# The output product by Strassen's identity over pairs of batches, in a phase of its own

## The chip, the core and the metric

The kernel runs on one core of a Trainium2 chip. TensorE (PE) multiplies; VectorE (DVE), ScalarE (ACT) and GpSimd (POOL) do the element-wise work; SyncE (SP) issues the DMA transfers. The metric is the device time of one execution in microseconds, as the median of several runs.

## The reference

An attention between 8 batches of 512 tokens and 32 state rows makes 4,352 rows of 512, which go through two gated feed-forward blocks:

```python
def _moe_ref(x, w1, w2, w3, w_out):
    a = x @ w1
    b = x @ w2
    h = a * b @ w3
    return (h @ w_out).astype(np.float32)

def _moe2_ref(x, w_in, w_out):          # w_in 512 x 2048, w_out 2048 x 512
    h = x @ w_in
    relu6 = np.clip(h + 3.0, 0.0, 6.0)
    g = h * relu6 / 6.0
    return (g @ w_out).astype(np.float32)
```

The change is in the second block: `h = x @ w_in` is the hidden product, `g` the gates, `g @ w_out` the output product. All of it is float32. Each factor is split into a rounded part and the rest (`rnd` on ACT, `rest` on DVE or POOL), and a product is three matmuls: high by high, high by low, low by high.

## The kernel before

**Three stages.** A first stage unpacks weights and begins the attention; then one slot after another (`slot`, 8 a batch) makes the first block's rows, which go to DRAM as `x2d[b]`, 512 channels by 512 tokens. In the first batches of this stage `stream2` unpacks `moe2_w_in` and `moe2_w_out` a little in each slot, and writes split weights to DRAM: `swi`, which is `w_in` as the seven weight combinations of Strassen's identity in eight groups of 128 hidden columns, and `swo`, which is `w_out` as it is. The last stage, from 553.8 us in the trace, is the second block, and the change is about it.

**The second block before.** It works on four pairs of batches, `p`. The 2 x 2 blocks of Strassen's identity are two halves of the hidden columns by two halves of the channels (of `w_in`), and two halves of the channels by the two batches (of `x`). `combos(p)` makes the seven combinations of the activations (`xc`: B11, T1, T2, B21, T3, B22, T4) from four loads `r` of `x2d`, a piece each time that the main loop steps it; for the pairs behind the first, four of the seven `rest` operations run on POOL. For each of 8 groups `n`, seven calls of `prod` (L799) do 6 matmuls of 128x128 by 512 columns each into three banks; ACT and DVE combine them to four blocks of hidden values, and `chain` (L812) makes gates of them: relu on ACT, the gate on DVE, `rnd` on ACT, `rest` on DVE.

**The output product before.** The gates of group `n - 1` are the stationary factor of `out_mm` (L840): for each batch and each quarter of the tokens, 6 matmuls of 512 columns against `wo`, 48 a group. They stand between the products of group `n`, one `out_mm` behind each (`T_`). Each result is added on DVE to an accumulator `oa` in SBUF, and after 8 groups the eight accumulators go to DRAM in rows of 2 KB. Rows of the 256 state rows go along in the last pair (`state_h`, and `out_mm` with `j == "s"`).

**What sets the order.** It is written by hand; every engine takes its instructions in the order of the code, and waits by semaphores. SP takes the DMAs likewise. Two buffers hold each tile of weights; a group's `w_load` and `wo_load` (896 KB twice and 512 KB twice) are issued when a group is done.

Of the kernel before, what the change touches and what calls it, by code (L numbers as in the profile page):

```python
# [7 lines left out]
F32 = mybir.dt.float32  # L8
# [11 lines left out]
def attn_moe_kernel(tc, xt_d, xn_d, bd_d, wa, wb, wc, wi, wo, out):  # L20
# [95 lines left out]
    swo = [[dram.tile([128, 2, 512], F32, name=f"swo{hl}{u}") for hl in "hl"] for u in range(8)]  # L116
# [223 lines left out]
    with tc.manual_schedule():  # L340
# [85 lines left out]
        def stream2():  # L426
# [22 lines left out]
            for i, (src, u) in enumerate(units):  # L449
# [26 lines left out]
                a11, a12, a22, a21 = (w[:, 256 * k:256 * k + 256] for k in range(4))  # L476
                s1, s2, s3, s4 = (cm[:, 256 * k:256 * k + 256] for k in range(4))
# [3 lines left out]
                yield  # L481
# [7 lines left out]
                for hl, t in enumerate((h, l)):  # L489
                    nc.sync.dma_start(out=swi[u][hl].rearrange("p s k f -> p (s k f)"), in_=t.bitcast(F32))  # L490
# [92 lines left out]
        def x2_load(p):  # L583
            if p < B // 2:
                x2r[p] = r = [xb.tile([128, 2, 512], F32, tag=f"r{i}", name=f"r{i}") for i in range(4)]
                for i in range(4):
                    nc.sync.dma_start(out=r[i], in_=x2d[2 * p + i % 2][:, i // 2 * 2:i // 2 * 2 + 2, :])

        def combos(p):

            if p >= B // 2:
                return
            b11, b12, b21, b22 = x2r.pop(p)

            def split(k, x, eng):
                t = xb.tile([128, 2, 2, 512], F32R, tag="xc", name="xc", bufs=8)
                h, l = xc[p, k] = t[:, 0], t[:, 1]
                rnd(h, x, "A")
                rest(l, x, h, eng)

            def minus(out_, a, b):
                nc.vector.tensor_tensor(out=out_, in0=a, in1=b, op=ALU.subtract)
            e = "VP"[p > 0]
            split("B11", b11, e)
            yield
            minus(b11, b12, b11)
            yield
            split("T1", b11, "V")
            yield
            minus(b11, b22, b11)  # L610
            yield
            split("T2", b11, "V")
            yield
            split("B21", b21, e)
            yield
            minus(b12, b22, b12)
            yield
            split("T3", b12, e)
            yield
            split("B22", b22, e)  # L620
            yield
            minus(b21, b21, b11)
            yield
            split("T4", b21, "V")
            if p:
                x2_load(p + 1)
            yield
# [86 lines left out]
        for b in range(B):  # L714
# [20 lines left out]
            for m in range(0 if b else 4, M1):  # L735
# [40 lines left out]
        LAST = NG * (B // 2)  # L776
        wts, wos = {}, {}

        def w_load(n):
            if n <= LAST:  # L780
                wts[n] = [pb.tile([128, 7, 2, 128], F32R, tag=f"w{hl}", name=f"w{hl}", bufs=2) for hl in "hl"]
# [106 lines left out]
        def state_h(n, i):  # L888
            if i == 0:
                ps_s[n] = bank("ps_hs")  # L890
# [153 lines left out]
```

## Time and profile before

| | us |
|---|---|
| median of 3 runs | 1265.66 |
| lowest, highest | 1263.24, 1265.81 |
| the profiled execution: device time | 1263.66 |
| the profiled execution: span from the first to the last instruction | 1261.7 |
| busy in the span: PE, DVE, ACT, POOL | 1225.7, 857.5, 518.5, 32.1 |

The span is 1.96 us shorter than the device time of the same execution. A busy PE is not PE at its peak, since matmuls overlap: how fast they follow each other is read from the chain, where one of 512 columns counts 0.23 us, though its own row says 390 ns. DVE and ACT instructions overlap by some 0.08 us as well; what one costs a full queue is the distance between two starts.

### The profile page before, as it was taken

Reading aid. Unit: us, or ns where it says so; the run is one execution under the profiler, and the core shown is the slowest. Engines: PE = TensorE matmul, PEld = TensorE weight load, DVE = VectorE, ACT = ScalarE, POOL = GpSimd, SP = SyncE. Lnnn points to the kernel's source line nnn. Section 1 sums busy time; section 2 is a strip of 40 time slices with the busy share of each in tenths; the row PEclk is TensorE's granted clock in tenths of the full one; section 3 lists DMA queues with packets and bytes.
Section 4 is the critical chain, followed back from the end, with each engine's and each line's share of the span. In section 5 each row is a group of like instructions: output and inputs, shape, how many; then the busy total and the mean of one; then the engine's idle time right before and its main releaser. Section 6 shows DMA issues by size and latency. Waiting matters only on the chain.

```text
span 1261.7 us, 16840 instructions
## 1 busy us (share of the span) xinstructions
PE 1225.7 (97%) x6784; PEld 970.1 (77%) x6784; DVE 857.5 (68%) x1268; ACT 518.5 (41%) x811; POOL 32.1 (3%) x18
## 2 busy tenths in 40 slices
PE   5989999999999999999999999999999999999997
PEld 2446787777778778778888888888888888888885
DVE  7976877786877642645667947679566697556664
ACT  3434545454654533444333543234423344332330
POOL 0000000000000000000000200002000030000000
PEclk9989999999999999999999999999999999999999
DMA  9751554554554201445525553445624254332223
GB/s 354 277 179 68 204 211 178 203 211 173 200 198 165 101 20 49 149 148 207 183 93 183 201 208 125 150 149 192 235 109 182 94 192 167 135 141 93 92 92 117
DMA packets 49589, 202.67 MB, mean 161 GB/s; under 512 B 9192, under 2 KB 11240, under 8 KB 42856
## 3 DMA queue, kind: packets, MB, share of 16 engines
q1 hardware_dynamic: 48936, 200.56, 43.8%
q8 instruction: 53, 0.87, 0.3%
q10 hardware_dynamic: 576, 1.05, 0.2%
q14 instruction: 24, 0.20, 0.0%
HBM read 160.17 MB, written 41.42 MB: 160 GB/s over the span
## 4 chain that ended last, share of the span: by engine, by line
PE 85%; DVE 10%; ACT 2%; DMA 1%; issue 1%; ACTq 0%; DVEq 0%; SPq 0%
PE ps L804 24%; PE ps_o L88 10%; PE ps_o L90 10%; PE ps_o L89 10%; PE x L88 4%; PE x L89 4%; PE x L90 4%; PE ps_ab L88 4%; PE ps_ab L90 4%; PE ps_ab L89 4%; PE ps_p L360 2%; PE ps_hs L804 2%; PE ps_w L414 1%; PE ps_r L228 1%; DVE ab L508 1%
## 5 line engine op out<-in xcount | busy, mean ns | idle before, releaser
L804 PE MATMUL ps<-xc,wh 128*128 128x512 f32 x896 | 276.1, 390 | 0.0
L808 DVE TENSOR_TENSOR oa<-oa,ps_o 128x512 f32<-128x512 f32 x238 | 163.0, 686 | 157.1 <-PE ps_o L90 156.3
L88 PE MATMUL ps_o<-woh,g 128*128 128x512 f32 x512 | 199.8, 390 | 0.3 <-ACT g L71 0.3
L89 PE MATMUL ps_o<-wol,g 128*128 128x512 f32 x512 | 199.7, 390 | 0.0
L90 PE MATMUL ps_o<-woh,g 128*128 128x512 f32 x512 | 199.6, 390 | 0.0
L804 PEld LDWEIGHTS ps<-xc,wh 128*128 128x128 f32 x896 | 168.3, 188 | 34.8
L804 PE MATMUL ps<-xc,wl 128*128 128x512 f32 x448 | 174.6, 390 | 0.0
L71 ACT ACTIVATE g<-gt 128x512 fp32r<-128x512 f32 x128 | 81.0, 632 | 173.0 <-DVE gt L818 172.9
L88 PE MATMUL x<-abh,w3ph 128*128 128x512 f32 (+1 forms) x288 | 112.4, 390 | 0.0
L90 PEld LDWEIGHTS ps_o<-woh,g 128*128 128x128 f32 x512 | 96.2, 188 | 20.5 <-DVE g L79 0.4
L88 PEld LDWEIGHTS ps_o<-woh,g 128*128 128x128 f32 x512 | 96.2, 188 | 20.1 <-ACT g L71 0.8
L89 PEld LDWEIGHTS ps_o<-wol,g 128*128 128x128 f32 x512 | 96.2, 188 | 19.3
L89 PE MATMUL x<-abl,w3ph 128*128 128x512 f32 (+1 forms) x288 | 109.1, 379 | 0.0
L90 PE MATMUL x<-abh,w3pl 128*128 128x512 f32 (+1 forms) x288 | 109.0, 378 | 0.0
L88 PE MATMUL ps_ab<-Ah,ph 128*128 128x512 f32 x256 | 102.7, 401 | 1.6 <-DVE pl L79 0.9
L90 PE MATMUL ps_ab<-Ah,pl 128*128 128x512 f32 x256 | 100.7, 394 | 1.7 <-DVE pl L79 1.7
L79 DVE TENSOR_TENSOR g<-gt,g 128x512 fp32r<-128x512 f32 x128 | 90.1, 704 | 17.9 <-ACT g L71 15.6
L89 PE MATMUL ps_ab<-Al,ph 128*128 128x512 f32 x256 | 100.6, 393 | 0.0
L804 PEld LDWEIGHTS ps<-xc,wl 128*128 128x128 f32 x448 | 84.1, 188 | 17.6 <-DMA wl<-swil 0.2
L71 ACT ACTIVATE abh<-ab 128x512 fp32r<-128x512 f32 (+1 forms) x72 | 43.7, 608 | 114.7 <-DVE ab L508 114.7
L815 ACT ACTIVATE rl<-c,half 128x512 f32<-128x512 f32 x96 | 69.4, 723 | 32.6 <-DVE c L808 31.2
L79 DVE TENSOR_TENSOR abl<-ab,abh 128x512 fp32r<-128x512 f32 (+1 forms) x72 | 47.4, 658 | 39.9 <-ACT abh L71 39.9
(122 smaller groups left out, 1724.2 us busy)
## 6 DMA issues: line engine op xcount, KB each, us to landing
wh<-swih SPq DMA_DIRECT2D x33, 896.0 KB, 4.6
wl<-swil SPq DMA_DIRECT2D x33, 896.0 KB, 6.4
woh<-swoh SPq DMA_DIRECT2D x33, 512.0 KB, 5.3
wol<-swol SPq DMA_DIRECT2D x33, 512.0 KB, 6.2
out_dram<-oa SPq DMA_DIRECT2D x34, 256.0 KB, 2.4
raw<-in_wb_dram SPq DMA_DIRECT2D x8, 1024.0 KB, 6.3
xr<-in_xt_dram SPq DMA_DIRECT2D x8, 1024.0 KB, 6.4
xn<-in_xn_dram SPq DMA_DIRECT2D x8, 1024.0 KB, 8.1
```

Of the source, the lines that this page charges most:

```text
L71: nc.scalar.activation(out=out_, in_=in_, func=AF.Copy)
L79: e.tensor_tensor(out=out_, in0=in_, in1=hi.bitcast(F32), op=ALU.subtract)
L88: nc.tensor.matmul(ps, lh, rh, start=first, stop=False)
L89: nc.tensor.matmul(ps, lh, rl, start=False, stop=False)
L90: nc.tensor.matmul(ps, ll, rh, start=False, stop=last)
L228: nc.tensor.matmul(ps[h:h + 64, c * NS:(c + 1) * NS], xn[:, t, c * 128 + h:c * 128 + h + 64], e2t[:, t, g, o:o + NS], start=(t == 0), stop ...
L360: nc.tensor.matmul(ps[c][32 * q:32 * q + 32, 256 * i:256 * i + 256], st_t[b][r, 2 * c + j, 32 * k:32 * k + 32], w12[mm // 2, 2 * c + j][r, ...
L414: nc.tensor.matmul(w3_ps[m], t[:, o:o + 128], wout[k], start=k == 0, stop=k == M1 - 1)
L508: nc.vector.tensor_tensor(out=ab[:, :n], in0=psb[:, :n], in1=a[:, :n], op=ALU.mult)
L804: nc.tensor.matmul(ps, u[:, a, k, :], v[:, k, :], start=first and k == 0 and i == 0, stop=k == 1 and i == 2, skip_group_check=not first or ...
L808: nc.vector.tensor_tensor(out=out_, in0=a, in1=b, op=ALU.add)
L815: nc.scalar.activation(out=rl, in_=c, func=AF.Relu, bias=half, scale=1.0 / 6.0)
```

## The change

**Products in two phases.** For each pair the hidden product of all 8 groups comes first (`hidden`), as seven calls of `prod` a group, and its gates stay in SBUF, unsplit, in four tiles `G[k][j]` of 8 x 512 (half `k` of the hidden columns, batch `j`). Then comes the output product (`output`), by the same identity: the 2 x 2 blocks are two halves of the 512 output channels by the two halves of the hidden columns (of `w_out`), and the gates. It goes through 28 steps `v`: seven products `i`, each in four steps `u` of 12 matmuls (two groups of hidden columns by two quarters `q` of 64 channels of either half). Here the weights are stationary, the gates move, and the result is transposed: channels by tokens.

**The gates' combinations.** The four sums of the identity are made in place on DVE, half a tile (2,048 columns) at a time (`t_sum`), and the two parts of a step's gates just before their use (`make`: `rnd` on ACT, `rest` on DVE, 1,024 columns) in a ring of three tiles `hl`. `make(v + 2)` stands behind step `v`; three of the 28 are made in the hidden phase.

**The way out.** At the end of a product (`ended`) DVE combines banks, and transposes 32 x 32 blocks (`put`) into `stg`; four DMAs write it in runs of 256 B. There is no accumulator `oa`.

**The activations.** `combos(p + 1)` runs in the output phase of pair `p`, one piece a step, in two halves of the channels (512 columns each instead of 1,024); each half begins with its load (`x2_load(p, k)`, 2 x 512 KB into the one buffer `r`), at steps 1 and 13. All its `rest` operations are on DVE, none on POOL.

**The weights.** `stream2` treats `w_out` as it treats `w_in`, so `swo` grows from 1,024 to 1,792 columns a group, and is stored by four DMAs a group instead of two. `STEPS` gets one more step in every fourth slot. Weights are loaded in units of 4 and 3 tiles of 256 columns (`w_load`, `w_done`), each with two buffers.

**The state rows.** Their hidden products stay in the last pair's groups, their output products (matmuls of 256 columns) go into steps of four of the seven products there.

The token order in the layout on the host changes with it. The diff, cut:

```diff
-    swo = [[dram.tile([128, 2, 512], F32, name=f"swo{hl}{u}") for hl in "hl"] for u in range(8)]
+    swo = [dram.tile([128, 7, 8, 256], F32, name=f"swo{hl}") for hl in "hl"]
...
-                if src is wo:
-                    rnd(h[:, :1024], w, "A")
-                    rest(l[:, :1024], w, h[:, :1024], "V")
-                    for hl, t in enumerate((h, l)):
-                        nc.sync.dma_start(out=swo[u][hl].rearrange("p k e -> p (k e)"), in_=t[:, :1024].bitcast(F32))
-                    yield
-                    continue
-
...
-                yield
...
                 for hl, t in enumerate((h, l)):
-                    nc.sync.dma_start(out=swi[u][hl].rearrange("p s k f -> p (s k f)"), in_=t.bitcast(F32))
+                    to = swi[u][hl].rearrange("p s k f -> p s (k f)") if src is wi else swo[hl][:, :, u, :]
+                    for at, of, n in ((0, 2, 5), (5, 0, 2)):
+                        nc.sync.dma_start(out=to[:, at:at + n, :],
+                                          in_=t.bitcast(F32)[:, 256 * of:256 * (of + n)].rearrange("p (s e) -> p s e", e=256))
...
-        def x2_load(p):
-            if p < B // 2:
-                x2r[p] = r = [xb.tile([128, 2, 512], F32, tag=f"r{i}", name=f"r{i}") for i in range(4)]
-                for i in range(4):
-                    nc.sync.dma_start(out=r[i], in_=x2d[2 * p + i % 2][:, i // 2 * 2:i // 2 * 2 + 2, :])
+        def x2_load(p, k):
+            r = x2r[p, k] = xb.tile([128, 2, 2, 512], F32, tag="r", name="r")
+            for j in range(2):
+                nc.sync.dma_start(out=r[:, :, j, :],
+                                  in_=x2d[2 * p + j].rearrange("p (h k) f -> p h k f", k=2)[:, :, k, :])
...
+            for k in range(2):
+                x2_load(p, k)
+                yield
+                r = x2r.pop((p, k))
...
+                def split(name, x):
+                    if k == 0:
+                        t = xb.tile([128, 2, 2, 512], F32R, tag="xc", name="xc", bufs=7)
+                        xc[p, name] = t[:, 0], t[:, 1]
+                    h, l = (x_[:, k] for x_ in xc[p, name])
+                    rnd(h, x, "A")
+                    rest(l, x, h, "V")
+
+                def minus(out_, a, b):
+                    nc.vector.tensor_tensor(out=out_, in0=a, in1=b, op=ALU.subtract)
+                split("B11", b11)
...
-                for _ in range(STEPS):
+                for _ in range(STEPS + (m % 4 == 3)):
...
-                    if m == 0:
-                        x2_load(0)
-                    else:
-                        next(first, None)
+                    for _ in range(1 if m == 0 else 4):
                         next(first, None)
...
+        def w_done(u):
+            wu.pop(u)
+            w_load(u + 4)
...
+        def t_sum(i, h):
+
+            a = 4 * h
+            b11, b12, b21, b22 = (G[k][j][:, a:a + 4, :] for k in range(2) for j in range(2))
+            if i == 1:
+                sub(b11, b12, b11)
+            elif i == 2:
+                sub(b11, b22, b11)
+            elif i == 4:
+                sub(b12, b22, b12)
+            else:
+                sub(b11, b21, b11)
+
...
+                if old is not None:
+                    o2, om1, ow = old
+                    prod(o2, ow(A22), X("T4"), False)
+                    w_done(2 * (base + n - 1) + 1)
+                    tick()
+                    c21 = small("c", 3)
...
+                prod(d3, w(S1), X("T1"), True)
+                tick()
+                m5 = small("m5", 2)
+                nc.scalar.copy(out=m5, in_=d3)
+                if with_states and n == 0:
+                    states_split()
+                early(n, 0)
+                prod(d1, w(A12), X("B21"), False)
+                tick()
+                chains.append(chain(d1, [(G[0][0][:, n, :], 0, 512)]))
+                early(n, 1)
+                prod(d2, w(S3), X("T3"), False)
+                tick()
                 c22 = small("c", 3)
...
+                add(c22, d2, m1)
+                add(c22, c22, m5)
+                chains.append(chain(c22, [(G[1][1][:, n, :], 0, 512)]))
...
+        def put(c, q, stg):
+            nc.vector.transpose(out=stg[:, :, q, :], in_=c)
...
+        def out_of(p, eh, j, stg):
+
+            blk = 2 * p + j
+            for g in range(4):
+                e = 128 * g + 64 * eh
+                nc.sync.dma_start(
+                    out=out[blk * ROWS:blk * ROWS + S, e:e + 64].rearrange("(b t) e -> t b e", t=32),
+                    in_=stg[32 * g:32 * g + 32].rearrange("p b q e -> p b (q e)"))
...
+            def make(v):
+                if v < 28 and v not in made:
+                    made.add(v)
+                    i, u = divmod(v, 4)
+                    split(two(ring[v % 3]), g_of(i, 2 * u, 2))
...
+            SUMS = {2: (1, 1), 4: (2, 0), 6: (2, 1), 9: (4, 1), 11: (6, 0), 13: (6, 1)}
...
+                def main():
+                    for q in range(2):
+                        for k in range(2):
+                            n = 2 * u + k
+                            wh, wl = (t[:, 128 * q:128 * q + 128] for t in w_at(base, 8 * i + n))
+                            for z, (a, x) in enumerate(((wh, hl[0]), (wh, hl[1]), (wl, hl[0]))):
+                                nc.tensor.matmul(d[name][q], a, x[:, k, :], start=i < 3 and n == 0 and z == 0,
+                                                 stop=n == NG - 1 and z == 2, skip_group_check=True)
...
+                for s in (8 * i + 2 * u, 8 * i + 2 * u + 1):
+                    if s % 7 == 3:
+                        w_done(2 * (base + s // 7))
+                    elif s % 7 == 6:
+                        w_done(2 * (base + s // 7) + 1)
+                make(v + 2)
+                if v in SUMS:
+                    t_sum(*SUMS[v])
+                if u == 3:
+                    ended(i)
+                side(v)
...
+            def early(n, k):
+                if last:
+                    return
+                if k == 0 and n in (3, 5, 7):
+                    u = (n - 3) // 2
+                    split(two(ring[u]), g_of(0, 2 * u, 2))
+                if k == 1 and n == 6:
+                    t_sum(1, 0)
+                if k == 1 and n == 7:
+                    t_sum(4, 0)
+            hidden(p, early)
...
+                gen = combos(p + 1)
+                per = {v: 1 for v in range(1, 28)}
+
+                def side(v):
+                    for _ in range(per.get(v, 0)):
+                        next(gen, None)
+            output(p, ring, (0, 1, 2), side)
```

**DVE, around the end of a hidden phase and the start of an output phase.** Before, one group's work between two products reads so (`oa` is an accumulator of the output, `g` a part of the gates, `u`, `m` and `c` combinations of the product's banks):

```order
L808 TENSOR_TENSOR u_6011<-ps_6004,m_5985 128x512
L808 TENSOR_TENSOR oa<-oa,ps_o 128x512 x2
L818 SCALAR_TENSOR_TENSOR gt<-rl,ps_5977 128x512
L808 TENSOR_TENSOR u_6045<-ps_6004,m_5985 128x512
L808 TENSOR_TENSOR c<-u_6045,m_5994 128x512
L808 TENSOR_TENSOR oa<-oa,ps_o 128x512
L79 TENSOR_TENSOR g_6058<-gt,g_6057 128x512
L818 SCALAR_TENSOR_TENSOR gt<-rl,c 128x512
```

Now, in the last group of the first pair's hidden phase, and on into its output phase (`hlj` is a tile of the ring, the rows of 2,048 columns are `t_sum`, `c<-ps_5682` reads the bank that the last product of the group adds to):

```order
L803 TENSOR_TENSOR u_5716<-ps_5682,m_5693 128x512
L820 SCALAR_TENSOR_TENSOR g_5144<-rl,c 128x512
L79 TENSOR_TENSOR hlj<-g_5142,hlj 128x1024
L806 TENSOR_TENSOR g_5143<-g_5145,g_5143 128x2048
L803 TENSOR_TENSOR c<-ps_5682,m_5693 128x512
...
L79 TENSOR_TENSOR hlj<-g_5142,hlj 128x1024 x2
L806 TENSOR_TENSOR g_5142<-g_5143,g_5142 128x2048
L79 TENSOR_TENSOR xc<-r,xc 128x512
L79 TENSOR_TENSOR hlj<-g_5142,hlj 128x1024
L600 TENSOR_TENSOR r<-r 128x512
```

The additions to `oa` and the `rest` of every gate are gone; two long instructions stand ahead of the read of the bank, and in the output phase every second instruction belongs to the next pair's activations, behind their load `r`.

**SP, around the loads of the next pair's activations.** Before, the four loads of a pair's end stand together, between rows of the output:

```order
L783 DMA wh<-swih_89 128x1792
L783 DMA wl<-swil_90 128x1792
L789 DMA woh<-swoh_103 128x1024
L789 DMA wol<-swol_104 128x1024
L863 DMA out_dram<-oa 128x512
L587 DMA r_7716<-x2d_83 128x1024
L587 DMA r_7717<-x2d_84 128x1024
```

Now, in the first steps of the first pair's output phase (`wah` to `wbl` are the units of weights):

```order
L785 DMA wbh<-swoh 128x768
L785 DMA wbl<-swol 128x768
L785 DMA wah<-swoh 128x1024
L785 DMA wal<-swol 128x1024
L580 DMA r<-x2d_79 128x2x512
L580 DMA r<-x2d_80 128x2x512
```

The loads of `r` are of the pair that comes next, stand behind the unit that step 1 releases, and their data are wanted one step later.

## Rows read from the trace of the kernel before

**Rows 1.** Busy time by stretch: us, each engine's busy us (instructions), clock, DMA, GB/s

```profile
100.00:450.00 350.00, 346.65 (x2564) 264.24 (x2563) 264.81 (x398) 181.44 (x297) 0.00 (x0) 1.00 0.47 172
450.00:553.80 103.80, 100.06 (x732) 85.63 (x731) 46.68 (x63) 39.16 (x67) 0.00 (x0) 1.00 0.21 71
553.80:1252.90 699.10, 698.73 (x3169) 581.41 (x3168) 463.85 (x695) 258.65 (x396) 31.37 (x12) 1.00 0.43 156
...
1252.90:1261.70 8.80, 0.00 (x0) 0.00 (x0) 0.68 (x1) 0.00 (x0) 0.00 (x0) 0.75 0.19 60
```

**Rows 2.** What PE waited for from 553 us on: us, times, longest

```profile
PE ps_o L88 <- ACT g L71: 0.3, 1, 0.3
```

**Rows 3.** Groups of PE instructions by shape: count, busy us, mean ns

```profile
L804 PE MATMUL ps<-xc,wh 128*128 128x512 f32 x896 | 276.1, 390 | 0.0
L88 PE MATMUL ps_o<-woh,g 128*128 128x512 f32 x512 | 199.8, 390 | 0.3 <-ACT g L71 0.3
...
L804 PE MATMUL ps<-xc,wl 128*128 128x512 f32 x448 | 174.6, 390 | 0.0
L804 PE MATMUL ps_hs<-xsB,wh 128*128 128x256 f32 x96 | 17.9, 283 | 0.0
...
L88 PE MATMUL ps_o<-woh,gs 128*128 128x512 f32 x32 | 12.5, 390 | 0.0
```

**Rows 4.** The chain that ended last, in order: start us, us, what

```profile
1217.10 1.36 PE ps L804 x6
...
1225.26 1.43 PE ps_hs L804 x12
```

**Rows 5.** Groups of DVE and ACT instructions by shape, columns as in rows 3

```profile
L808 DVE TENSOR_TENSOR oa<-oa,ps_o 128x512 f32<-128x512 f32 x238 | 163.0, 686 | 157.1 <-PE ps_o L90 156.3
...
L71 ACT ACTIVATE xc<-r 128x1024 fp32r<-128x1024 f32 x28 | 29.4, 1054 | 13.1 <-DVE r L602 13.1
...
L602 DVE TENSOR_TENSOR r<-r,r 128x1024 f32<-128x1024 f32 x16 | 19.5, 1217 | 0.1
...
L937 ACT COPY m<-ps 128x512 f32<-128x512 f32 x32 | 18.7, 585 | 17.2 <-PE ps L804 17.2
...
L260 DVE STREAM_TRANSPOSE aT<-sN 128x512 f32<-128x512 f32 x16 | 10.4, 687 | 0.0
...
L79 DVE TENSOR_TENSOR sl<-w,sh 128x768 fp32r<-128x768 f32 x8 | 7.6, 946 | 0.0
...
L480 DVE TENSOR_TENSOR cm<-w 128x256 f32<-128x256 f32 x8 | 3.4, 419 | 0.0
```

**Rows 6.** DVE in order of time: start us, us, instruction

```profile
692.82 1.22 DVE L602 TENSOR_TENSOR r<-r,r 128x1024 f32<-128x1024 f32 x1
693.96 0.68 DVE L808 TENSOR_TENSOR u<-ps,m 128x512 f32<-128x512 f32 x1
694.56 0.68 DVE L808 TENSOR_TENSOR oa<-oa,ps_o 128x512 f32<-128x512 f32 x1
```

**Rows 7.** SP's queue in order of time, a load of weights

```profile
743.78 0.32 SPq L783 DMA_DIRECT2D wh<-swih  x1
744.19 0.38 SPq L783 DMA_DIRECT2D wl<-swil  x1
```

**Rows 8.** DMA issues by line: count, KB each, median us from issue to landing

```profile
wl<-swil SPq DMA_DIRECT2D x33, 896.0 KB, 6.4
...
out_dram<-oa SPq DMA_DIRECT2D x34, 256.0 KB, 2.4
...
r<-x2d SPq DMA_DIRECT2D x16, 512.0 KB, 5.8
...
xsd<-xs SPq DMA_DIRECT2D x8, 64.0 KB, 2.5
```

**Rows 9.** Busy time by stretch, while that load's data moved

```profile
745.00:750.00 5.00, 5.00 (x24) 4.15 (x23) 2.70 (x5) 3.87 (x7) 0.00 (x0) 1.00 0.93 361
```

**Rows 10.** DVE in order of time, its last instruction

```profile
1252.89 0.69 DVE L808 TENSOR_TENSOR oa<-oa,ps_o 128x512 f32<-128x512 f32 x1 [0.67 <-PE ps_o L90]
```

**Rows 11.** PE in order of time, early in the kernel

```profile
67.47 1.92 PE L360 MATMUL ps_p<-big,br 64*32 64x256 f32 x22 [3.73 <-DVE big L155]
```

**Rows 12.** Busy time by stretch, around that wait

```profile
66.00:80.00 14.00, 10.14 (x71) 5.55 (x72) 12.39 (x17) 6.23 (x10) 0.00 (x0) 0.63 0.67 226
```

More of the change, by code (lines that the diff above doesn't have):

```diff
@@ L807, in add, with sub, small @@
         def add(out_, a, b):
             nc.vector.tensor_tensor(out=out_, in0=a, in1=b, op=ALU.add)
-        G, chains = {}, []
-        def chain(key, c):
-            rl = pb.tile([128, 512], F32, tag="rl", name="rl", bufs=2)
+        def sub(out_, a, b):
+            nc.vector.tensor_tensor(out=out_, in0=a, in1=b, op=ALU.subtract)
+        def small(tag, bufs, name=None):
+            return pb.tile([128, 512], F32, tag=tag, name=name or tag, bufs=bufs)
+        G = [[pb.tile([128, NG, 512], F32, name=f"g{k}{j}") for j in range(2)] for k in range(2)]
@@ L826, in chain @@
-            G[key] = h, l
-            rnd(h, gt, "A")
-            yield
-            rest(l, gt, h, "V")
+            for o, a, n in outs:
+                nc.vector.scalar_tensor_tensor(out=o, in0=rl[:, a:a + n], scalar=1.0, in1=c[:, a:a + n], op0=ALU.min,
+                                               op1=ALU.mult)
         def tick():
@@ new lines, in two, with split, g_of @@
+        def two(t):
+            return t[:, 0], t[:, 1]
+        def split(hl, x):
+            rnd(hl[0], x, "A")
+            rest(hl[1], x, hl[0], "V")
+        ORDER2 = [(0, 0), (0, 0), (0, 0), (1, 1), (0, 1), (1, 0), (0, 0)]
+        def g_of(i, a, n):
+            k, j = ORDER2[i]
+            return G[k][j][:, a:a + n, :]
+        def t_sum(i, h):
[7 more added lines that the diff above has]
+                sub(b12, b22, b12)
+            else:
+                sub(b11, b21, b11)
@@ new lines, in prod, with hidden @@
+        def prod(ps, w, x, first):
+            h, l = (t.rearrange("p (k f) -> p k f", k=2) for t in w)
+            for k in range(2):
+                for i, (u, v) in enumerate(((h, x[0]), (h, x[1]), (l, x[0]))):
+                    nc.tensor.matmul(ps, u[:, k, :], v[:, k, :], start=first and k == 0 and i == 0,
+                                     stop=k == 1 and i == 2, skip_group_check=True)
+        def hidden(p, early):
+            base = 2 * NG * p
+            with_states = p == PAIRS - 1
+            old = None
@@ new lines, in nothing, with side @@
+        def nothing(*_):
+            pass
+        for p in range(PAIRS):
+            last = p == PAIRS - 1
+            ring = None if last else jit_tiles(pb, "hl", 3, 3)
+            def early(n, k):
+                if last:
+                    return
+                if k == 0 and n in (3, 5, 7):
[6 more added lines that the diff above has]
+            hidden(p, early)
+            if last:
+                ring = jit_tiles(xb, "xc", 3, 7)
+                sa, sd = ([xb.tile([128, NG, 256], F32R, tag="xc", name="sx", bufs=7) for _ in range(2)] for _ in range(2))
+                st["hl"] = {0: sa, 1: sa, 5: sa, 6: sd}
+                g1, g2 = st["G"]
+                for u in range(3):
+                    split(two(ring[u]), g_of(0, 2 * u, 2))
+                    if u == 0:
+                        tick()
+                        split([t[:, :4] for t in sa], g1[:, :4])
+                tick()
+                split([t[:, 4:] for t in sa], g1[:, 4:])
+                t_sum(1, 0)
+                t_sum(4, 0)
+                todo = {8: lambda: sub(g1, g2, g1), 10: lambda: split(sa, g2), 14: lambda: split(sd, g1)}
+                def side(v):
+                    todo.get(v, nothing)()
+            else:
+                gen = combos(p + 1)
+                per = {v: 1 for v in range(1, 28)}
+                def side(v):
+                    for _ in range(per.get(v, 0)):
+                        next(gen, None)
+            output(p, ring, (0, 1, 2), side)
+            if not last:
+                for _ in gen:
+                    pass
+                if p == PAIRS - 2:
+                    states_x()
```

394 lines of the change are left out of this document (191 added, 203 removed).

## The prediction

> **What bounds the kernel now.** I read the busy time by stretch first. From 553.8 to 1252.9 us, the whole second block, PE is busy 698.73 of 699.10 us at clock 1.00, while DVE is busy 463.9, ACT 258.7 and the DMA engines 0.43 of it [rows 1]. The list of waits has 0.3 us for PE in all that time [rows 2]. So the second block lasts as long as its matmuls, and nothing else in it costs a microsecond. Next the count of matmuls: 896 + 448 of the hidden product (`ps`), 3 x 512 of the output product (L88; L89 and L90 are alike) and 3 x 32 of the state rows' output, all of 512 columns: 2,976; and 192 of 256 columns (`ps_hs`, of which the largest group is shown) [rows 3]. The chain of waits gives the price: six of 512 columns in 1.36 us, 0.2267 each; twelve of 256 in 1.43 us, 0.119 each [rows 4]. 2,976 x 0.2267 + 192 x 0.119 = 697.5 us, against 699.1 measured. So a matmul less is 0.227 us less, as long as PE keeps waiting for nothing. That is what has to be examined.
>
> **What goes.** The output product falls from 1,536 to 4 x 28 x 12 = 1,344 matmuls of 512 columns; the state rows' 96 of 512 become 192 of 256. What is left in the block is 1,344 + 1,344 = 2,688 and 384: 609.3 + 45.8 = 655.1 us. Against 697.5 that is **-42.4 us**.
>
> **DVE, in total.** The price of one in a full queue is the distance of two starts: 0.60 us for 512 columns, 1.14 for 1,024 [rows 6]. For 2,048 columns no row stands; 256, 512 and 1,024 take 0.42, 0.69 and 1.22 us [rows 5], so 2,048 take about 2.27, and 2.20 in a full queue (an estimate). An output phase of the first three pairs has 25 `rest` of the ring (28.5), 6 half sums (13.2), 22 operations of `combos` of 512 columns (13.2), and 18 adds and transposes at the ends of products (0.60 each, 10.8; the transposes of before cost as much as an add, 0.69 us [rows 5], and the strided `stg` has no row: I take the same, at twice it would be 4.8 us more a phase). Together 66 us, against 28 x 12 x 0.2267 = 76.2 us of PE. So DVE doesn't become the bound; it fills 86% of the phase, and what matters is where it comes late. In the hidden phases PE has 8 x 9.5 us and DVE some 58; ACT is lighter everywhere.
>
> **Where PE will wait.** PE runs ahead of DVE by the ring: `make(v + 2)` lets it have two steps, 5.4 us, in hand. I carried the instructions forward in their order, engine by engine, with these prices and 0.1 us for a hand-off.
>
> First, the last group of a hidden phase. Counted from the end of its S1 product: ACT copies m5 (0.5) and rounds the third ring tile (0.97 [rows 5, 6]), DVE makes its rest (1.14) and the half sum behind it (2.20), and only then reads the bank of S2 and S3 (0.6): 5.9 us. The product T4 adds to that bank, and there is no next group left to stand between, so PE is there after three products, 4.1 us. It waits 1.8. Three pairs.
>
> Second, step 5 of an output phase. The load of the next pair's activations is issued when step 1 ends, 5.4 us into the phase, behind the unit of weights that step 1 released: 2.1 MB. Before, 1.83 MB (`wh`, `wl`) were issued 0.41 us apart, and the second landed 6.4 us later [rows 7, 8], 6.8 in all; at 0.36 to 0.40 MB/us [rows 9] the rest takes 0.7: 7.5 us. Loads of 512 KB alone take 5.8 [rows 8]; these are the two ends, and I take 7.2, since the weights do stand ahead. So the data is there at 12.7. `rnd` of B11 waits for it in ACT's queue at step 2, and the rounding for step 5 stands behind it (0.55 + 0.97), then its rest on DVE (1.14), with hand-offs 15.7. PE has done step 4 at 13.6, and one matmul can go on the rounded part: it waits 1.8.
>
> Third, DVE then has no slack until it has caught up, and the half sums of steps 4, 6 and 11 push it behind PE again: 0.5, 0.2 and 0.7 us at steps 7, 9 and 14. Fourth, the second half's load, issued when DVE has read the last of `r` (step 12): it lands around step 16, with the same chain behind it, and the four instructions at the end of product 3 follow: 0.5 at step 17, 1.7 at step 18, and 0.6 at step 22 behind the six of product 4. That is 8.0 us for each of three pairs, **24 us**.
>
> The last pair has no `combos`, but its ring is made only behind its last product: an add and a rest, 1.9 us. The state rows' load and split cost about 1.1 in its first group, the state products 0.25 in each of the next seven, steps 14 and 18 together 1.0: **5.8 us**. A unit of weights of the first pair comes 0.6 late, as its DMA is issued behind the ones that write `x2d`. Sum of the waits: **30.4 us**. The ends are 10 (loads in 5.8 us, ring never late again) and 60 (loads 2 us later than taken: 6 of them, and 3 us more in the last pair, and `stg` at twice).
>
> **The slots ahead of it.** Eight units of `wo` now get four DVE operations of 256 columns (0.42) and a longer rest (0.95 more), 2.6 us each, 21 us in all. In the slots DVE is busy 265 of 350 us and PE waits 3.4 [rows 1]: it is hidden by DVE's 85 idle us, and costs at worst all 21. I take 1.0. `combos(0)` in half pieces costs no more than before and lies beside a full PE.
>
> **DMA and the end.** Weights come at 1.83 MB per group of 9.5 us, 0.19 MB/us, half the rate of [rows 9], and 13.6 us before they are wanted; hidden, unless the stores hold them up. These are 2,048 runs of 256 B four times a pair. The nearest row is `xsd`: 512 runs of 128 B land in 2.5 us, as 256 KB in long rows do in 2.4 [rows 8]. By that 2,048 cost between 1.3 us (their bytes) and 10 (four times it); slack is about 8, so 0 to 30 us in all, and I take 0. At the end, before, a last add followed PE [rows 10] and 8.8 us passed to the end of the span [rows 1]; now two adds, two transposes and four DMAs: some 2.6 + 2.1 + 2.5 + 0.8 = 8.0. That is -0.8.
>
> **The sum.** Against the profiled execution: 1263.7 - 42.4 + 30.4 + 1.0 - 0.8 = 1251.9. It lies 2.0 below the median, but within the three runs; from the parts (553.8 + 1.0 + 655.1 + 30.4 + 8.0 + 1.96) it is 1250.3. I take **1251**, with 1240 to 1260 as the range of this case. Chance 0.6.
>
> **Rivals.** The waits stay hidden: the loads land in 5.8 us, DVE's starts overlap the waits, and only 10 to 15 us remain: 1231 to 1236. For it: DVE is 14% idle in the phase, and PE now waits for nothing. Against it: the two orders above are fixed, and two of the waits hang on no load. Chance 0.2.
>
> The slots take the work badly, and half to all of its 21 us comes out: 1260 to 1272. Chance 0.08, half of it within 0.2% of no change or slower.
>
> Slower than before: the load of `r` comes 2 us later than I take, so that PE waits 3.8 us at steps 5 and 17 of three pairs. The trace has such a wait: 3.73 us for DVE [rows 11], and in the 14 us from there on the granted clock was 0.63 on average [rows 12], part of it at 1.2 instead of 2.4 GHz; 14 x 0.37 = 5 us lost. Waits of up to 2 us at 450 to 553.8, 3.7 us in all, left it at 1.00 [rows 1]. Six times 2 + 5 us is 42, hence 1293. It decides from about 1 us of lateness on, where some of the six fall, and at half of them the gain is gone. For it: no row shows these loads behind weights; against it: 0.43 DMA load. Chance 0.09. The Trainium skill ("TensorE: Matmul & The Clock Gate", section "HAM oscillation — how this bites in real kernels") says the same of a loop that waits for a load between bursts of matmuls: each burst begins at the slow clock. By that rule even my waits might count, if they lie close; the stretch at 450 to 553.8 speaks against it.
>
> That the change doesn't do what it says is excluded by the order of its instructions: 2,688 and 384 matmuls stand there. The remaining 0.03 is for what I don't see, to either side.
>
> **How the numbers follow.** Likeliest 1251. Below 1231 I leave 0.07, above 1266 0.11. 0.2%, about what a measurement of this kernel can tell from no change, is 2.5 us. Faster: 0.6 + 0.2 + half of the slots' case and a little = 0.86; same: 0.05; slower: 0.09.
>
> **What would show it.** In the profile after: PE busy by the matmuls some 655 us of a second block of about 686; its waits for `rest` of ring tiles (DVE) at steps 5, 17 and 18, for the bank of T4 at the last group, none for weights; hidden phases of 76 to 78 us and output phases of 82, the last pair's 102 each; `r` landing in 6 to 7.5 us; the clock at 1.00 throughout. I am wrong if the output phases take 76 or 90, if the clock falls in them, or if PE waits for `wah` to `wbl`.

## The result, and the profile after

The changed kernel takes **1275.68 us**, the median of 4 runs (1273.1 to 1277.73); the kernel before took 1265.74 beside it (1263.24 to 1266.18). The ratio is 1.0082, 95% interval 1.0058 to 1.0105: it is slower by 10 us, and I forecast 1251 and faster. The profiled execution spans 1271.3 us. It shows one part near the forecast and one far from it.

The busy time by stretch, of the changed kernel (us, each engine's busy us and instructions, clock, DMA share, GB/s); these rows answer to [rows 1]:

```profile
100.00:450.00 350.00, 332.58 (x2441) 253.66 (x2440) 271.72 (x422) 177.00 (x290) 0.00 (x0) 0.98 0.54 190
...
575.90:1265.10 689.20, 668.75 (x3074) 550.97 (x3072) 490.40 (x596) 286.17 (x380) 0.00 (x0) 1.00 0.59 192
1265.10:1271.30 6.20, 0.00 (x0) 0.00 (x0) 1.33 (x3) 0.00 (x0) 0.00 (x0) 0.82 0.57 130
```

The second block begins at 575.9 us instead of 553.8 and lasts 695.4 to the end of the span, where it lasted 707.9. So the block itself gained 12.5 us; the forecast for it was 655.1 + 30.4 + 8.0 = 693.5. But 22.1 us were lost ahead of it, in the slots, for which I had taken 1.0. There PE is busy 332.6 of 350 us, where it was busy 346.7.

What PE waited for most in the slots (100 to 450 us; total, times, longest), of the changed kernel:

```profile
PE ps_e L213 <- ACT asb L500: 16.5, 5, 3.3
```

In the kernel before, the same transposes `ps_e` of attention waited 2.5 us in three times, for DVE's `ab`. Now they wait 3.3 us, once in each of five batches, 58 us apart. What follows each wait is seen in the busy time of the 3.4 us behind the first three of them:

```profile
173.40:176.80 3.40, 3.40 (x13) 2.75 (x12) 2.70 (x5) 2.88 (x6) 0.00 (x0) 0.50 0.33 137
231.40:234.80 3.40, 3.36 (x12) 2.99 (x13) 2.70 (x6) 2.59 (x6) 0.00 (x0) 0.50 0.42 176
289.40:292.80 3.40, 3.16 (x12) 2.80 (x13) 2.70 (x5) 2.58 (x6) 0.00 (x0) 0.51 0.51 214
```

The granted clock is 0.50, 1.2 instead of 2.4 GHz, so up to 1.7 us (half of 3.4) are lost each time on top of the wait. At 347.5 and 405.5 us, behind the other two, it is 0.50 as well, and so it is at 507.9 us, behind shorter waits. What all this costs is read from the whole time ahead of the second block, of the kernel before and then of the changed kernel:

```profile
0.00:553.80 553.80, 527.01 (x3616) 388.69 (x3617) 392.96 (x573) 259.89 (x415) 0.70 (x6) 0.99 0.46 168
```

```profile
0.00:575.90 575.90, 534.45 (x3616) 395.76 (x3617) 413.38 (x624) 266.55 (x430) 0.70 (x6) 0.97 0.48 171
```

PE does the same 3,616 matmuls. It is idle for 41.4 us instead of 26.8, 14.7 more, of which the five waits less the 2.5 us of before are 14.0; and it is busy 7.4 us longer, at a mean clock of 0.97 instead of 0.99. Together they are the 22.1. The Trainium skill ("TensorE: Matmul & The Clock Gate", section "HAM oscillation — how this bites in real kernels") describes this pattern for a loop that waits for a load in each round, with some 1.67 us of slow clock in each; here the wait is for DVE and ACT, and the rows show 3.4 us.

The wait itself, in the first of the five batches, in order of time: PE, then ACT, then DVE (start us, us, instruction, idle before and what ended it):

```profile
173.15 1.91 PE L213 MATMUL ps_e<-ident,e 128*128 128x128 f32 x8 [3.29 <-ACT asb L500]
```

```profile
171.78 0.84 ACT L71 ACTIVATE sh<-w 128x768 fp32r<-128x768 f32 x1 [4.25 <-issue]
172.53 0.57 ACT L500 COPY asb<-ps_ab 128x512 f32<-128x512 f32 x1
```

```profile
165.16 0.68 DVE L502 TENSOR_TENSOR ab<-ps_ab,asb 128x512 f32<-128x512 f32 x1
165.76 1.21 DVE L251 TENSOR_REDUCE sm<-sN 128x32 f32<-128x1024 f32 x1
...
168.08 1.22 DVE L256 TENSOR_TENSOR sN<-sN,sm 128x1024 f32<-128x1024 f32 x1
169.22 1.22 DVE L458 SCALAR_TENSOR_TENSOR w<-raw,ts 128x1024 f32<-128x1024 uint32 x1
170.47 1.23 DVE L463 TENSOR_TENSOR w<-w,hd 128x1024 f32<-128x1024 f32 x1
171.73 0.43 DVE L471 TENSOR_TENSOR cm<-w 128x256 f32<-128x256 f32 x1
...
173.20 0.68 DVE L502 TENSOR_TENSOR ab<-ps_ab,asb 128x512 f32<-128x512 f32 x1
```

From the product `ab` of slot 3 (165.16) to that of slot 4 (173.20) DVE has no idle time that the trace lists. Attention's sum, reciprocal and product stand there, and behind them three steps of `stream2` at once: `w` (L458), its addition (L463) and the four combinations. ACT stands idle for 4.25 us ahead of its rounding of `w`; the trace puts no releaser to it (`issue`), but the rounding reads the `w` of L463 and starts 0.08 us after L463 ends (171.70). Behind it in ACT's queue stands the copy `asb`, which reads the bank that PE waits for.

### The profile page after: what moved, and what is told of

The parts are those of the page before. It is cut to its first block, busy times and chain, and to the rows that moved or that the text cites. A ratio compares the mean times of both kernels' runs of the same rounds, so it can differ in the third digit from the quotient of the medians.

```text
span 1271.3 us, 17016 instructions
## 1 busy us (share of the span) xinstructions
PE 1203.2 (95%) x6688; PEld 946.7 (74%) x6688; DVE 905.1 (71%) x1221; ACT 552.7 (43%) x809; POOL 0.7 (0%) x6
## 4 chain that ended last, share of the span: by engine, by line
PE 65%; DVE 21%; ACT 5%; DMA 4%; issue 4%; ACTq 0%; SPq 0%; DVEq 0%
PE ps L886 22%; PE ps_d L1052 13%; PE x L88 4%; PE x L89 3%; PE x L90 3%; DVE hlj L79 3%; DVE g L806 3%; PE ps_ab L90 3%; PE ps_ab L88 3%; PE ps_ab L89 3%; PE ps_hs L886 2%; DMA r<-x2d 2%; PE ps_so L1065 2%; PE ps_p L360 2%; PE ps_w L414 1%
## 5 line engine op out<-in xcount | busy, mean ns | idle before, releaser
L886 PE MATMUL ps<-xc,wah 128*128 128x512 f32 x512 | 158.1, 390 | 0.0
L1052 PE MATMUL ps_d<-hlj,wah 128*128 128x512 f32 x384 | 122.9, 396 | 6.7 <-DVE hlj L79 5.8
L886 PE MATMUL ps<-xc,wbh 128*128 128x512 f32 x384 | 118.7, 390 | 7.6 <-DVE c L803 4.9
L79 DVE TENSOR_TENSOR hlj<-g,hlj 128x1024 fp32r<-128x1024 f32 x84 | 102.5, 1220 | 25.2 <-ACT hlj L71 25.0
L886 PEld LDWEIGHTS ps<-xc,wah 128*128 128x128 f32 x512 | 95.9, 188 | 19.4
L71 ACT ACTIVATE hlj<-g 128x1024 fp32r<-128x1024 f32 x84 | 87.9, 1056 | 38.1 <-PE ps_d L1052 32.1
L886 PE MATMUL ps<-xc,wal 128*128 128x512 f32 x256 | 99.6, 389 | 0.0
L1052 PEld LDWEIGHTS ps_d<-hlj,wah 128*128 128x128 f32 x384 | 72.5, 189 | 28.3 <-DVE hlj L79 11.7
L1052 PE MATMUL ps_d<-hlj,wbh 128*128 128x512 f32 x288 | 90.7, 394 | 2.6 <-DVE hlj L79 1.5
L502 DVE TENSOR_TENSOR ab<-ps_ab,asb 128x512 f32<-128x512 f32 x64 | 44.0, 688 | 45.5 <-PE ps_ab L90 41.5
L1052 PE MATMUL ps_d<-hlj,wal 128*128 128x512 f32 x192 | 75.1, 391 | 0.0
```

The lines of the kernel that those rows point to most:

```text
L71: nc.scalar.activation(out=out_, in_=in_, func=AF.Copy)
L79: e.tensor_tensor(out=out_, in0=in_, in1=hi.bitcast(F32), op=ALU.subtract)
L502: nc.vector.tensor_tensor(out=ab[:, :n], in0=psb[:, :n], in1=a[:, :n], op=ALU.mult)
L886: nc.tensor.matmul(ps, u[:, k, :], v[:, k, :], start=first and k == 0 and i == 0, stop=k == 1 and i == 2, skip_group_check=True)
L1052: nc.tensor.matmul(d[name][q], a, x[:, k, :], start=i < 3 and n == 0 and z == 0, stop=n == NG - 1 and z == 2, skip_group_check=True)
```

## The experiments

**Three readings of that wait.** Theory A: it is ACT's order, the rounding that stands ahead of `asb`. Theory B: the 21 us of added DVE work have to be paid, wherever they stand. Theory C: it is the stores, now in more and smaller pieces. Three runs, beside the kernel before at 1264.2 us.

First, the rounding a step later:

```
-                rnd(h[:, :768], w[:, :768], "A")
                 ... (four combinations)
                 yield
+                rnd(h[:, :768], w[:, :768], "A")
                 rnd(h[:, 768:], cm, "A")
```

> The rounding of w (ACT, `sh<-w`) is issued one step of `stream2` later; nothing is left out, all of the added work of `wo` stays. Theory A (ACT's queue order: in the slot whose three steps hold stt, add and rounding, ACT stands 4.25 us for DVE's w with the next slot's copy of `asb` behind it, and PE waits 3.29 us for that copy, in five batches): the five waits of PE for `asb` fall below 1 us each, the five stretches of halved clock behind them go, the second block begins at 553 to 559 us instead of 575.9, total 1253 to 1260. Theory B (the 21 us of added DVE work have to be paid wherever they stand): block from 570 to 577, total 1271 to 1277. Theory C (the stores in four pieces instead of two, 45,024 short packets): as B.

Measured: 1278.74 us, ratio 1.0114 (1.0089 to 1.0139). PE's waits in the slots, then PE and DVE in order of time at the first of them, of this run:

```profile
PE ps_e L213 <- DVE ab L502: 17.7, 5, 3.6
```

```profile
174.07 1.11 PE L213 MATMUL ps_e<-ident,e 128*128 128x128 f32 x4 [3.58 <-DVE ab L502]
```

```profile
173.33 0.68 DVE L502 TENSOR_TENSOR ab<-ps_ab,asb 128x512 f32<-128x512 f32 x1
```

ACT's rounding is gone from the place, and the wait is as long as it was: now it is put down to DVE's own `ab`, which reads the same banks and stands at the same time, 173.3. Theory A falls. ACT had only been the last of two that were late for one reason, the queue of DVE.

Second, the two extra steps of a batch behind slots 1 and 5, `STEPS + (m % 4 == 1)`:

> The two extra steps of `stream2` in each batch stand behind slots 1 and 5 instead of 3 and 7; nothing is left out, work and order within a unit are as in the changed kernel. The three-step slots then hold addition, rounding and rest, or the reverse end of a unit, never stt, addition and rounding together. Theory A: ACT waits for w only as long as one addition, so PE's waits for `asb` come out at 0 to 2 us instead of 3.29, total 1254 to 1266. Theories B and C: the same sum of work and stores per batch, total 1272 to 1278.

Measured: 1269.26 us, 1.0038 (1.0025 to 1.0051), between what A and B say. The waits of PE for `asb` in the slots come to 10.6 us, five of them, the longest 2.3. The work is that of the changed kernel, and only its place differs: that speaks against B, though A's range isn't met either.

Third, the units of `wo` as before, with as many bytes stored (two steps a slot again, and the combinations of `wi` in two steps again, a `yield` not shown here):

```
+                if src is wo:
+                    rnd(h[:, :1024], w, "A")
+                    rest(l[:, :1024], w, h[:, :1024], "V")
+                    ... (seven slices of each stored), yield, continue
-                for _ in range(STEPS + (m % 4 == 3)):
+                for _ in range(STEPS):
```

> The units of `wo` are treated in `stream2` as in the kernel before (five steps, no combinations, two steps a slot); the combinations of w_out are left out, so the output product multiplies other slices, with as many bytes stored as in the changed kernel. Theories A and B: the second block begins at 553 to 556 us and lasts 695, total 1249 to 1254. Theory C (stores): 560 to 576, total 1257 to 1276, since the bytes of the stores are those of the changed kernel. All: the second block itself is unchanged, 694 to 697 us.

Measured: 1251.54 us, 0.9902 (0.9886 to 0.9919); the second block begins at 554.0. The slots read as they did before the change:

```profile
100.00:450.00 350.00, 346.65 (x2564) 263.87 (x2563) 265.05 (x398) 181.48 (x297) 0.00 (x0) 1.00 0.54 190
```

PE is busy 346.65 us, as in [rows 1], with the DMA share of the changed kernel (0.54). So the bytes stored cost nothing, and theory C falls: all of the loss hangs on the work on `wo` in the slots, or on the steps in which it stands. The total is within 1 us of the forecast.

**Theory D: DVE's work in one slot.** What the runs so far have in common is the slot of attention's product. From the start of one `ab` (L502) to the start of the next, DVE works without a break for 8.04 us there in the changed kernel (PE waits 3.3), 6.79 with the extra steps elsewhere (2.1 to 2.3), and 6.0 to 6.5 in batches 1 to 5 of the kernel before (at most 1.1). The 7.57 and 6.35 of the next expectation are another count, some 0.5 us shorter. If that is so, the same 18 steps a batch have a place where they cost nothing, and work that costs nothing on average costs all of itself in that slot. Four runs test it; in the first two the only edit is the number of steps behind each slot:

```
-                for _ in range(STEPS + (m % 4 == 3)):
+                for _ in range(((3, 2, 2, 1, 2, 2, 3, 3) if b else (0, 0, 0, 0, 2, 2, 3, 2))[m]):
```

> The same 18 steps of `stream2` a batch, spread as 3, 2, 2, 1, 2, 2, 3, 3 over slots 0 to 7 instead of 2, 2, 2, 3, 2, 2, 2, 3; nothing is left out. Theory D, formed after the runs on the rounding and on slots 1 and 5: the slot in which attention's sum, reciprocal and product (3.0 us) stand has 7.57 us of DVE work with three steps, PE has some 5.4 us of work there and waits 3.3, with two steps 6.35 and 2.3; so it is DVE's work in this one slot that counts. With one step it is some 4.65 us: PE's wait for the banks falls to between 0 and 1.1 us (as in the kernel before), no halved clock behind it, block from 553.5 to 558, total 1249 to 1255. Theory B (the sum of DVE's work in a batch counts): 1268 to 1278.

Measured: 1251.88 us, 0.9902 (0.9887 to 0.9917), beside 1263.63; the second block begins at 553.2. DVE in that slot, and what is left of PE's wait:

```profile
163.59 0.68 DVE L502 TENSOR_TENSOR ab<-ps_ab,asb 128x512 f32<-128x512 f32 x1
...
166.51 1.23 DVE L256 TENSOR_TENSOR sN<-sN,sm 128x1024 f32<-128x1024 f32 x1
167.65 1.22 DVE L463 TENSOR_TENSOR w<-w,hd 128x1024 f32<-128x1024 f32 x1
168.79 0.68 DVE L502 TENSOR_TENSOR ab<-ps_ab,asb 128x512 f32<-128x512 f32 x1
```

```profile
PE ps_e L213 <- DVE ab L502: 0.2, 1, 0.2
```

One step instead of three, 5.2 us from one `ab` to the next instead of 8.04, and 16.5 us of waits have become 0.2. Every instruction is still there: ahead of the second block DVE is busy 412.3 us with 624 instructions (413.4 and 624 in the changed kernel), in 553.2 us instead of 575.9.

> As the spread run, but 3, 3, 2, 0, 2, 2, 3, 3 steps, none behind the slot of attention's product; nothing is left out. Theory D: DVE has 3.4 us there, no wait is left at that place, but the addition to w that moves to slot 2 puts DVE's product of slot 3 some 0.4 us later: total as the spread run within 3 us, 1248 to 1256. Theory B: 1268 to 1278.

Measured: 1252.61 us, 0.9909 (0.9894 to 0.9924), the spread run within what the two can tell apart. One step there is few enough.

The other two are done on the kernel before, so that nothing of the change is in them. Two sums that nobody reads are added behind a slot, in five batches:

```
+                if 0 < b < B - 2 and m == 3:      (m == 6 in the second)
+                    for _ in range(2):
+                        nc.vector.tensor_reduce(out=scr, in_=w12[0, 0]..., op=ALU.add, axis=AX.X)
```

> The kernel before, with two sums over 128x1024 (some 1.2 us each, as attention's L251) on DVE whose result nobody reads, behind slot 3 of batches 1 to 5: 12 us of DVE work in all, nothing else changed. Theory D (DVE's work in the slot of attention's product counts): DVE has 5.3 to 5.6 us there, then some 7.9; PE waits 2 to 4 us for the banks in four or five batches, and falls to the halved clock behind some of them, 1.7 us each: total 1272 to 1290. Theory B' (DVE's 85 idle us of 350 hide what is added, as the prediction had it): 1263 to 1267.

> The kernel before with the same two sums, 12 us of DVE work in all, behind slot 6 of batches 1 to 5, where PE has 8 to 8.7 us of work and DVE 5.5 to 6.1. Theory D: DVE's work there grows to 8.0 to 8.5 us and stays inside the slot: total 1263 to 1268, no long wait. A theory by which any 12 us on DVE cost as much: as the run with the sums behind slot 3.

Measured, beside 1263.97: behind slot 3, 1281.72 us, 1.0139 (1.0124 to 1.0154); behind slot 6, 1264.49, 1.0004 (0.9995 to 1.0013). PE's waits for `ab` in the slots, of the first and of the second:

```profile
PE ps_e L213 <- DVE ab L508: 13.1, 5, 3.5
```

```profile
PE ps_e L213 <- DVE ab L508: 2.5, 3, 1.1
```

The same 12 us of DVE work cost 17.7 us in one slot and 0.5 in another, which is within the noise. Of the 17.7, 10.6 are longer waits; the clock was halved behind three of the five, for 6.8, 3.4 and 3.4 us. The busy time of one such slot, from `ab` to `ab`, shows why; first slot 3 of a batch in the first run, then slot 6 in the second:

```profile
219.70:228.10 8.40, 5.81 (x55) 4.06 (x53) 8.26 (x12) 1.22 (x2) 0.00 (x0) 0.99 0.54 218
```

```profile
180.50:189.20 8.70, 8.70 (x122) 6.87 (x121) 7.96 (x11) 2.57 (x5) 0.00 (x0) 1.00 1.01 357
```

Slot 6 has 8.70 us of PE work to lie beside; slot 3 has 5.81, and DVE's 8.26 set its length. Theory D stands, and B falls, with it the prediction's own reading (B' in the expectation).

**The waits of the second block.** Its sum came within 2 us; the runs ask whether its terms were right. Three are changed: the half sums of T1 and T4 in groups 5 and 6 instead of 6 and 7; the next pair's first load issued ahead of the hidden phase, `next(gen)` before `hidden(p, early)`; and no step of `combos` at steps 14 and 15, behind the second load.

> The half sums of T1 and T4 are issued one group earlier, in groups 5 and 6 of a hidden phase instead of 6 and 7; nothing is left out. My working of the second block (PE waits 1.8 us for the bank of T4 in the last group of three hidden phases because the half sum of 2.2 us stands ahead on DVE): the three waits go, -5.3 us, total 1268 to 1272, block from 575.9 as in the changed kernel. Rival (DVE's sum of work in the hidden phase is what is late, so the wait only moves a group ahead): the same time as the changed kernel, 1274 to 1277.

> The spread run (1251.9), with the next pair's first load issued before the hidden phase; the second load is issued at step 13 as before, and no step is left out behind it; nothing of the computation is left out. My working: only the waits at step 5, and those that DVE's lost slack brings at steps 7 to 14, go; the ones at 17, 18 and 22 stay: 5 to 9 us below the spread run, 1243 to 1247, against 16.5 with both. Rival: all of the gain came from the first load: 1234 to 1238.

> The spread run, and in it the next pair's first load of activations issued before the hidden phase instead of at step 1 of the output phase, and no step of `combos` at steps 14 and 15, so that the second load has two more steps to land; nothing is left out. My working of the prediction (the waits at step 5 and at steps 17 and 18 come from B11's rounding standing in ACT's queue until its load lands): waits of some 1.1 at step 5 and 2.1 at 17 and 18, three pairs, go: 5 to 10 us below the spread run. Rival: they come from DVE's sum of work in these steps (half sums, adds and transposes), whenever the load lands: 0 to 3 us below.

> As the run with the loads ahead, and the half sums of T1 and T4 one group earlier besides; nothing is left out. The wait for T4's bank went from 4.9 to 1.2 us in all where the half sums alone were moved: 3 to 5 us below the run with the loads ahead, some 1238 to 1247 in all. Rival: the half sums only move the wait to the ring tiles of the output phase: within 1.5 us of it.

Measured: the half sums alone on the changed kernel 1272.11 us, 1.0061 (1.0037 to 1.0084), an interval that overlaps that of the changed kernel. On the spread kernel (1251.88): the first load alone 1245.25, 0.9845 (0.9824 to 0.9866), as expected; both loads 1235.34, 0.9768 (0.9754 to 0.9783), which is 16.5 less where 5 to 10 was expected; and the half sums besides 1229.93, 0.9722 (0.9706 to 0.9738), 5.4 less where 3 to 5 was expected. What PE waited for in the second block of the changed kernel:

```profile
PE ps_d L1052 <- DVE hlj L79: 7.3, 10, 1.4
PE ps L886 <- DVE c L803: 4.9, 3, 1.6
PE ps L886 <- DVE u L803: 2.8, 1, 2.8
PE ps_d L1052 <- ACT hlj L71: 1.8, 3, 1.1
PE ps_d L1052 <- DVE xcj L79: 1.5, 2, 1.1
PE ps_hs L886 <- ACT xsB L71: 1.2, 1, 1.2
```

and of the run with all three edits:

```profile
PE ps L886 <- DVE u L803: 3.7, 1, 3.7
PE ps_d L1052 <- DVE xcj L79: 1.5, 2, 1.1
PE ps L886 <- DVE c L803: 1.2, 3, 0.4
```

The waits for ring tiles (`hlj`) are gone with the loads, and the three for T4's bank (`c`) fall from 4.9 to 1.2 with the half sums. The list explains only part of the gain of both loads: the `hlj` waits of the spread run were 9.7 of the 16.5. That the loads stood behind them is seen in ACT's queue of the changed kernel, in the first output phase:

```profile
669.75 0.63 ACT L71 ACTIVATE xc<-r 128x512 fp32r<-128x512 f32 x1 [5.75 <-DMA r<-x2d]
670.29 1.04 ACT L71 ACTIVATE hlj<-g 128x1024 fp32r<-128x1024 f32 x1
...
705.08 0.63 ACT L71 ACTIVATE xc<-r 128x512 fp32r<-128x512 f32 x1 [5.24 <-DMA r<-x2d]
705.62 1.99 ACT L71 ACTIVATE hlj<-g 128x1024 fp32r<-128x1024 f32 x2
```

**A wait that I had not seen.** The first group of the second block waits 2.8 to 3.9 us for `u` in all of these runs. DVE, then PE, of the run with all three edits:

```profile
563.59 0.69 DVE L803 TENSOR_TENSOR u<-ps,m 128x512 f32<-128x512 f32 x1 [11.17 <-DMA wbh<-swih]
```

```profile
564.34 1.02 PE L886 MATMUL ps<-xc,wbh 128*128 128x512 f32 x2 [3.66 <-DVE u L803]
```

`u` is read from a product that doesn't use `wbh`, and PE used `wbh` at 559.16, so it isn't the transfer named here. In the spread run the same wait is put down to the last stores of the slots:

```profile
DVE u L803 <- DMA x2d<-x2s: 10.7, 1, 10.7
```

In the run with all three edits the last of these stores was issued at 557.0 and took 6.3 us to land, until 0.3 us before `u`. My theory was the place of the tile: `u` lies where their staging `x2s` lay, and may be written only when the store has read it. Three lines that allocate `stg`, `c` and `rl` first move it:

```
+        pb.tile([128, 16, 2, 32], F32, tag="stg", name="stg")
+        small("c", 3)
+        small("rl", 2)
         for p in range(PAIRS):
```

> The run with both changes (1229.9), with the tiles of the first sums of the second block placed elsewhere in SBUF: they no longer lie where `x2s` lay, whose store to `x2d` DVE waited for (the first `u` stood 11 us on a DMA, PE 3.7 us for it); nothing of the computation is left out. Theory: the wait of 3.7 us and the halved clock behind it go: 1223 to 1227. Rival (the first unit of weights is as late as the store): 1228 to 1231.

Measured: **1227.23 us**, 0.9709 (0.9695 to 0.9724), 2.7 less. DVE's first `u` no longer waits for a transfer:

```profile
556.34 0.69 DVE L803 TENSOR_TENSOR u<-ps,m 128x512 f32<-128x512 f32 x1 [6.43 <-ACT m L907]
```

The wait is gone; the gain is half of what it and the clock behind it would have given, just outside the range. In this profile the clock is halved at 1024.5 us, where the run without the three lines had it halved at 564.6, behind the wait. This version is the fastest of all, 2.9% under the kernel before.

## Why the prediction was wrong, point by point

**The step that failed** is "it is hidden by DVE's 85 idle us, and costs at worst all 21. I take 1.0." The work was sized rightly: ahead of the second block DVE is busy 413.4 us instead of 393.0, 20.4 more. But the idle time was a sum over 350 us, and PE has only a few banks in hand: what DVE has to spare in slot 6 is of no use in slot 3. I wrote that the change puts one step more behind every fourth slot and never asked which steps meet which of attention's operations. With 18 steps a batch, three whole units, the same three steps (4.1 us of DVE) fell into the slot of attention's product (3.0 us) in each of five batches, whereas before, with 11 steps for two units and 16 a batch, the pattern moved on. The durations stood in the trace of the kernel before. What the runs showed in place of the 1.0 is 22.1 us: 14.7 of idle PE, and 7.4 by which the same matmuls took longer at the slower clock.

"At worst all 21" was no bound either: the waits alone stay below it, and with the clock behind them they pass it.

**The rival that came true in part** is "the slots take the work badly, and half to all of its 21 us comes out: 1260 to 1272", at 0.08. It had the right stage, but said nothing of how, and its price had no clock in it. The clock I had put into another rival, the one with late loads, which didn't come. There I had held the "waits of up to 2 us at 450 to 553.8", which left the clock at 1.00, against an early fall of the clock. That was weak: the trace lists single waits of at most 1.1 there, and behind the same waits the clock was halved in the spread run (last section).

**The matmuls** (-42.4 us) were right within some 6 us: with nearly all waits taken away, in the fastest version, PE is busy 660.9 of the 665.6 us of the second block, against 655.1 worked out; up to 1.7 of the difference is the slow clock at 1024.5. The row is the busy time of that block to PE's end:

```profile
553.40:1219.00 665.60, 660.88 (x3073) 551.29 (x3071) 490.32 (x595) 288.60 (x379) 0.00 (x0) 1.00 0.61 198
```

**The waits of the second block** (+30.4 us; the terms of a pair add up to 7.8 and not 8.0, 0.6 less in all): to PE's end it lasts 689.2 us, 34.1 over its matmuls. By terms: T4's bank, 1.8 in each of three pairs, was 4.9 by the list, and taking it away gave 5.4 us. The loads' waits, at steps 5, 7 to 14, 17, 18 and 22, were 18.6 for three pairs; taking both loads' lateness away gave 16.5, of it the first load 6.6. The loads landed in 6.4 us where I had taken 7.2, between 5.8 alone and 7.5 behind weights. The last pair's `hlj` and state terms show as `xcj`, `xsB` and their like, some 3 us of 5.8. Not foreseen were the 2.8 for `u`, and two stretches at half clock (869.7 and 1071.1), up to 1.7 us each; a clock that falls in an output phase, as at 869.7, was one of the prediction's signs of being wrong. The list holds 20 us of the 34; the rest lies in matmuls that the trace shows as longer, the slow clock among them, and I can't split it further. So the mechanism of these terms is shown, but that their sum came within 2 us of the block is in part luck.

**The end** was forecast as 8.0 us and is 6.2, the last row of the table by stretch.

**DMA**: 2,048 runs of 256 B were given 1.3 to 10 us, and 0 on the path. The four stores that write them took 2.5 each, and no wait of PE for weights is in the list.

```profile
r<-x2d SPq DMA_DIRECT2D x4, 512.0 KB, 6.4
out_dram<-stg SPq DMA_DIRECT2D x4, 128.0 KB, 2.5
```

(issues of the first output phase of the changed kernel, 655 to 715 us: count, KB each, median us to landing).

## What to carry to other kernels

Idle time of an engine may be set against added work only within the stretch that its buffers let the bottleneck run ahead: here one slot, some 5 to 9 us, not the 350 us of the stage. Before work is put between other work, lay the new pattern over the old slot by slot, and see whether the longest pieces of both meet; if the pattern has the period of the loop, they meet each time. When a wait is put down to one engine, ask what that engine was waiting for: taking ACT's rounding away moved the name of the releaser and not the wait.

## What the runs showed of the hardware

A wait of PE can cost more than itself. Behind waits of 3.3 us the granted clock was 0.50 for 3.4 us in every one of the five batches of the changed kernel. Other waits did the same less surely, and not by their length. With the extra steps behind slots 1 and 5, the five waits were 2.31, 2.07, 2.07, 2.06 and 2.08 us; the clock fell behind the second, fourth and fifth and stayed at 1.00 behind the longest. Two waits of 1.1 and 0.8 us close together stood ahead of such a stretch at 846.9 in the spread run, and hardly shorter ones (0.8 and 0.8) of the run with `wo` as before did not have it. The same two waits at the start of the state rows' product (0.7 and 1.1 us) left the clock at 1.00 in the kernel before, and it was 0.50 behind them in the spread run:

```profile
461.30:475.00 13.70, 11.94 (x76) 10.70 (x76) 3.42 (x5) 3.69 (x8) 0.00 (x0) 1.00 0.05 20
```

```profile
461.20:464.60 3.40, 3.40 (x18) 3.40 (x18) 0.00 (x0) 0.37 (x1) 0.00 (x0) 0.50 0.00 0
```

In the run with the rounding later, a wait of 3.5 us in the first group of the second block left the clock at 1.00:

```profile
583.00:595.00 12.00, 8.49 (x38) 6.70 (x37) 4.92 (x8) 3.10 (x5) 0.00 (x0) 1.00 0.76 248
```

So no length of a wait can be read from these runs that decides it, and a range for a forecast with waits of 1 to 4 us should hold up to 1.7 us more for each of them. In the second block this stayed small; ahead of it, it was 7.4 of 22 us.
